# LSH attention and mixture of experts on one core: the hash taken in fp32 from the turned q and k

## The chip, the cores and the metric

The kernel runs on one core of a Trainium2 chip. The metric is the device time of one execution in microseconds (us). The kernel before was timed three times: 741.52, 741.85 and 741.86 us, median 741.85. The core has five engines that matter here, each with its own queue that is worked off in order: TensorE (PE, its weight loads shown as PEld), VectorE (DVE), ScalarE (ACT), GpSimd (POOL) and SyncE (SP), which issues the DMAs.

## What is computed

There are 2 batches, 8 heads, 768 tokens and a head dimension of 64; the experts are 4, with 512 inputs and 1024 hidden units. A token's bucket is made of the signs of six projections of its q (or k), and attention is only between tokens of one bucket:

```python
q_bits = (np.einsum('bhsd,dk->bhsk', q, proj) > 0).astype(np.int64)
k_bits = (np.einsum('bhsd,dk->bhsk', k, proj) > 0).astype(np.int64)
q_bucket = np.sum(q_bits * powers, axis=-1)
k_bucket = np.sum(k_bits * powers, axis=-1)
mask = q_bucket[:, :, :, None] == k_bucket[:, :, None, :]
scores = np.where(mask, scale * np.matmul(q, k.transpose(0, 1, 3, 2)), -1e9)
attn = np.exp(scores - np.max(scores, axis=-1, keepdims=True))
attn = attn / (np.sum(attn, axis=-1, keepdims=True) + 1e-09)
x = np.matmul(attn, v)          # heads side by side: 1536 x 512
# experts, p = domain_probs / (sum + 1e-9)
for e in range(E):
    out += p[:, e:e + 1] * (np.maximum(x @ w1[e], 0.0) @ w2[e])
```

## The kernel before, in words

The sixteen heads are numbered 0 to 15 in the order (batch, head). Each is worked in six tiles of 128 queries; the tiles stand in one sequence of 48 per batch. For every step of the sequence the generator `attention` emits stages of several tiles in the order TXSUVMEYNRP, and every engine's queue keeps that order:

- S: four matmuls into `sps` (two banks of PSUM), the scores of a tile with the mask folded in by extra rows of `al` and `k2`; DVE then takes the row minimum and writes `p` (L391). `sps` has two buffers.
- E: ACT's exponential of the tile before (L407), with the row sum into `den`; the last tile of a head adds 1e-9 to `den` on ACT (L410).
- T (heads 0 to 8, called mixed): six PE transposes of the probabilities into two `ptps` banks, copied out by ACT, or by ACT and DVE (L458, L460). Heads 9 to 15 (light) instead turn 32x32 blocks on DVE (X) and go through a DMA to DRAM and back (`scr`, then `pt` in stage Y).
- V: the product with v, `pv` (L509): fp32 matmuls of 64 columns in pairs, one of a pair at column position 0 and one at 64, `LAG_V` steps after the head's last tile: two blocks of six matmuls at lags 4 and 6 for a mixed head, one of twelve at lag 7 for a light one. U copies `pv` out (`xf`), N takes the reciprocal of `den`, R spreads it by DMA, M multiplies it in on POOL.
- P: one piece of `prep_head` for the next head, a generator that is advanced once per step, so that each of its `yield`s moves what follows to the next tile.

`prep_head` makes the operands of the next head. q and k are loaded with 32-wide blocks side by side and turned by one DVE transpose into `xt` (q in partitions 0 to 63, k in 64 to 127), for the heads in `BLOCKS`; heads 9 and 10 are loaded plainly and turned by six PE transposes into `tps`. Then ACT writes the high part `ah` (scaled, rounded to fp32r, L230), DVE the low part `al` (L231), POOL copies parts of `ah` into `q1` and `k2` (L221). All this is in the head's tile 0. The hash of q and k with `proj` is six matmuls of 108 columns into two `hps` banks (L329): high data with the high and the low part of `proj`, low data with the high part; it stands two tiles later for a mixed head, one tile later for a light one. ACT's Sign (L316) writes the bits into `k2`, POOL scales them into `al` (L343) and copies twelve rows back.

`hps` and `tps` of these heads come from the pool of two double banks that `sps` uses too (tag `big`). The four single banks (tag `one`) serve `ptps`, `pv` and the experts' `mps`. Heads 0 and 1 are prepared by code of their own that the change leaves.

Batch 0 runs alone, with parts of the weights' splits between (DVE cast L683, POOL difference L676). From there the experts' matmuls for batch 0 (`mps`, L715 to L717 and L775 to L777) are emitted with the light heads of batch 1 among them: `prep_head`, S and T yield costs, and the attention is advanced whenever its costs fall behind the experts'. Then the experts for batch 1 run alone. Every DMA, the weights `ws` among them, is issued by SP in the order of emission.

Of the kernel before, what the change touches and what calls it, by code (L numbers as in the profile page):

```python
# [14 lines left out]
P = 128  # L15
# [3 lines left out]
SGN_SCALE = float(2**20)  # L19
ATT_PACE = 1.0  # L20
LAG_E = 1
LAG_N = 3
LAG_R = ((6, 4), (7, 6))
LAG_T = 3
LAG_X = 2
LAG_Y = 4
LAG_V = ((4, 6), (7,))
LAST_V = (4, 5)
LAG_U = (3, 1)
LAG_M = (10, 10)  # L30
PP_BUFS = 6
TW = 3
QK_AT = 1
BLOCKS = (2, 3, 4, 5, 6, 7, 8, 11, 12, 13, 14, 15)
W_LOAD = 14
W_BUFS = 2
WC = 2
# [12 lines left out]
def tile_lsh_attention__then__domain_moe(  # L50
# [59 lines left out]
    pr = const.tile([P, 2, NB], F32, name="pr")  # L110
    phi_t = const.tile([P, P], F32R, name="phi")
    plo_t = const.tile([P, P], F32R, name="plo")
    phi, plo = phi_t[:, :MKE], plo_t[:, :MKE]
    eps = const.tile([P, 1], F32, name="eps")
    warm = const.tile([P, 8], F32, name="warm")
    dp = const.tile([P, B, NT, E], F32, name="dp")
    dsum = const.tile([P, B, NT], F32, name="dsum")
# [2 lines left out]
    def two(t):  # L120
        return t.rearrange("p (a n) -> p a n", a=2)
# [26 lines left out]

    def setup():
        nc.vector.memset(warm, 0.0)  # L150
        nc.vector.memset(eps, 1e-9)
        nc.scalar.activation(warm[:, 0:1], warm[:, 0:1], ACTF.Exp)
        make_identity(nc, ident)
        keep_warm(N_WARM)
        step_column(qk_scale, ((0, -scale), (D, 1.0)))
        step_column(
            sgn_bias, ((0, -TINY), (MQ + NB, TINY), (MQE, 0.0), (MK, TINY), (MK + NB, -TINY), (MKE, 0.0))
        )
        step_column(bit_mul, ((0, 0.5), (MK, BIG / 2)))
        nc.vector.memset(phi_t.bitcast(F32), 0.0)  # L160
        nc.vector.memset(plo_t.bitcast(F32), 0.0)
        for i, s in ((0, -1.0), (1, 1.0)):
            hi, lo = (
                x[:, MQ:P].rearrange("p (a n) -> p a n", a=2)[:, :, i * NB : (i + 1) * NB] for x in (phi_t, plo_t)
            )
            nc.vector.tensor_scalar(out=hi, in0=pr, scalar1=s, scalar2=None, op0=ALU.mult)
            nc.vector.scalar_tensor_tensor(
                out=lo, in0=pr, scalar=s, in1=hi.bitcast(F32), op0=ALU.mult, op1=ALU.subtract
            )
# [17 lines left out]
    def in_blocks(b, h):  # L187
        return b * H + h in BLOCKS

# [99 lines left out]

    def prep_head(b, h):  # L290
        second = (b, h) == (0, 1)
        if not second and not in_blocks(b, h):
            tqk = loaded.pop((0, b, h))
        q1, al, ah, k2 = stack_tiles(b, h)
        if second:
            for ps, sl in zip(in_psum, halves):
                split_half(ah[:, sl], al[:, sl], ps[:, :NH])
        elif in_blocks(b, h):
            if (b, h) not in xts:
                turn_blocks(b, h)  # L300
                yield 0
            split_half(two(ah), two(al), two(xts.pop((b, h))))
        else:
            ps = big("tps")
            for c in range(NT):
                nc.tensor.transpose(
                    ps[:, c // 3, (c % 3) * P : (c % 3 + 1) * P], tqk[:, c].rearrange("p a d -> p (a d)"), ident
                )
            split_half(two(ah), two(al), ps[:, :, :NH])
        for rows in (slice(0, D), slice(D, P)):  # L310
            copy_pool(q1[rows], ah[0:D].bitcast(F32))
        copy_pool(k2[0:D], ah[D:P].bitcast(F32))
        yield 654

        def sign():
            nc.scalar.activation(  # L316
                two(k2[D:MKE]), hps[D:MKE, :, :NH], ACTF.Sign, bias=sgn_bias[D:MKE], scale=SGN_SCALE
            )

        if mixed(b, h) and (second or in_blocks(b, h)):  # L320
            yield 0
        if second:
            ps = [one("hps1") for _ in range(2)]
        else:
            hps = big("hps")
            ps = [hps[:, i] for i in range(2)]
        for j, (w, a) in enumerate(((phi, ah), (plo, ah), (phi, al))):
            for i, sl in enumerate(halves):
                nc.tensor.matmul(ps[i][:MKE, :NH], w, a[:, sl], start=j == 0, stop=j == 2)  # L329
        copy_pool(ah[0:D], al[D:P].bitcast(F32))  # L330
        if second:
            for i, sl in enumerate(halves):
                nc.scalar.activation(
                    k2[D:MKE, sl], ps[i][D:MKE, :NH], ACTF.Sign, bias=sgn_bias[D:MKE], scale=SGN_SCALE
                )
        if not mixed(b, h):
            sign()
        yield 978
        if b and h and not in_blocks(b, h):
            yield 0  # L340
        if mixed(b, h) and not second:
            sign()
        nc.gpsimd.tensor_scalar(  # L343
            out=al[D:MKE],
            in0=k2[D:MKE].bitcast(F32),
            scalar1=1.0,
            scalar2=bit_mul[D:MKE],
            op0=ALU.add,
            op1=ALU.mult,
        )  # L350
        copy_pool(k2[MQ:MQE], al[MK:MKE].bitcast(F32))
        yield 0

    xhi = {}
    xlo = {}
# [46 lines left out]
    def stage_e(b, h, t):  # L402
        pt, nb = probs_t[b, h, t]
        r, o, n = span_of(b, h, t)
        if o == 0:
            dens[b, h, r] = sm.tile([P, NT], F32, tag="den", name="den")
        nc.scalar.activation(pt, pt, ACTF.Exp, bias=nb, scale=-1.0, accum_out=dens[b, h, r][:, o : o + 1])  # L407
        if o == n - 1:
            den = dens[b, h, r][:, :n]
            nc.scalar.activation(den, den, ACTF.Identity, bias=eps)  # L410

    rdbs = {}
    rows = {}
# [1 line left out]
    def stage_n(b, h, t):  # L415
        r, o, n = span_of(b, h, t)
        if o != n - 1:
            return
        den = dens.pop((b, h, r))
        rd = sm.tile([P, NT], F32, tag="rd", name="rd", bufs=2)  # L420
        nc.vector.reciprocal(out=rd[:, :n], in_=den[:, :n])
        rows[b, h, r] = dr.tile([P, n], F32, tag=f"row{n}", name="row", bufs=6)
        nc.sync.dma_start(out=rows[b, h, r], in_=rd[:, :n])
# [149 lines left out]
    def attention():  # L573
# [3 lines left out]
        def do(op, i):  # L577
# [10 lines left out]
            elif op == "T":  # L588
                j = i - LAG_T
                if 0 <= j < n and heavy(*seq[j]):  # L590
                    stage_t(*seq[j])
                    return 654
            elif op == "X":
                j = i - LAG_X
                if 0 <= j < n and not heavy(*seq[j]):
                    stage_x(*seq[j])
            elif op == "Y":
                j = i - LAG_Y
                if 0 <= j < n and j % G == G - 1 and not heavy(*seq[j]):
                    b, h, t = seq[j]  # L600
                    stage_y(b, h, t // G)
            elif op == "S":
                if i < n:
                    b, h, t = seq[i]
                    if t == 0:
                        x = hseq.index((b, h))
                        prep[0] = prep_head(*hseq[x + 1]) if x + 1 < len(hseq) else iter(())
                    stage_s(b, h, t)
                    return 652 + 4270 // NT
                return DRAIN  # L610
            elif op == "V":
                for bh, lag in ended(i):
                    for part, at in enumerate(v_lags(*bh)):
                        if lag == at:
                            stage_v(*bh, part, len(v_lags(*bh)))
            elif op == "U":
                for bh, lag in ended(i):
                    if lag == u_lag(*bh):
                        stage_u(*bh)
            elif op == "M":  # L620
                for (b, h), lag in ended(i):
                    for g in range(NT // G):
                        if h % 2 and lag == (u_lag(b, h) if (b, h) == (0, H - 1) else LAG_M[b] + g):
                            stage_m(b, h, g)
            elif op == "E":
                j = i - LAG_E
                if 0 <= j < n:
                    stage_e(*seq[j])
            elif op == "P":
                if i < n:  # L630
                    b, h, t = seq[i]
                    c = next(prep[0], None) if t >= PREP_AT else None
                    x = hseq.index((b, h))
                    if t == NT - 1 and x + 2 < len(hseq) and in_blocks(*hseq[x + 2]) and mixed(*hseq[x + 2]):
                        turn_blocks(*hseq[x + 2])
                    if t == QK_AT and x + 2 < len(hseq):
                        load_qk(*hseq[x + 2])
                    if t == NT - 1 and x + 1 < len(hseq):
                        load_v(*hseq[x + 1])
                    return c  # L640
# [417 lines left out]
```

## Time and profile before

| what | value |
|---|---|
| median of three runs | 741.85 us |
| the profiled execution | 741.69 us, its span 740.0 us (1.7 us lie around it) |
| PE busy | 720.4 us, 97% of the span |
| PEld, DVE, ACT, POOL busy | 84%, 64%, 40%, 41% |
| the chain that ended last | PE 91%, ACT 4%, DVE 4% |
| waits of PE for another engine, largest | `hps` L329 for DVE p L391, 9.3 us |

"Busy" of PE counts a matmul from its start until its modelled end, so that matmuls that follow each other overlap; what a matmul takes of PE is read from the starts of neighbours. `pv` has two records in the trace for each matmul of the program (384 for 16 heads of twelve). The share of the span is an average over three stages: batch 0's attention alone until about 149 us, the experts of batch 0 with batch 1's attention until about 425 us, and the experts of batch 1.

### The profile page before, as it was taken

What the parts mean: (1) busy time and instruction counts of PE and PEld (TensorE: products, weight loads), DVE (VectorE), ACT (ScalarE), POOL (GpSimd) and SP (SyncE); (2) the same over time, 40 slices, a digit from 0 to 9 for tenths busy, and PEclk for the clock granted to TensorE, in tenths of its full rate; (3) what the DMA queues carried; (4) which work ended last, traced back from release to release, by engine and by line L of the source; (5) the groups of instructions that cost most, each with busy time, mean ns of one, the idle gap of its engine ahead of it and who ended that gap; (6) DMA issues with size and microseconds to landing.
All of it is one profiled execution on the core that took longest, in us unless ns stands there. A gap on an engine that the chain in (4) does not pass through costs nothing.

```text
span 740.0 us, 10166 instructions
## 1 busy us (share of the span) xinstructions
PE 720.4 (97%) x3826; PEld 618.4 (84%) x3826; DVE 474.5 (64%) x781; ACT 298.9 (40%) x592; POOL 306.3 (41%) x279
## 2 busy tenths in 40 slices
PE   8898889999999999999999999999999999999997
PEld 6666666698897897979779799998989989899896
DVE  6677776545776666667553334798668686676863
ACT  6676767643242241523312010443435334353440
POOL 5338585442335441644132324844234242343420
PEclk9999999999999999999999999999999999999999
DMA  6233324302877797789668211242121221212202
GB/s 143 44 65 66 79 43 101 74 13 69 208 203 177 216 229 189 194 209 280 173 196 231 83 58 57 72 157 85 48 67 58 85 86 34 81 57 78 93 0 86
DMA packets 85504, 83.05 MB, mean 112 GB/s; under 512 B 49872, under 2 KB 52432, under 8 KB 85456
## 3 DMA queue, kind: packets, MB, share of 16 engines
q1 hardware_dynamic: 84432, 82.08, 41.0%
q8 instruction: 30, 0.49, 0.3%
q10 hardware_dynamic: 1024, 0.33, 0.2%
q14 instruction: 18, 0.15, 0.1%
HBM read 62.68 MB, written 19.71 MB: 111 GB/s over the span
## 4 chain that ended last, share of the span: by engine, by line
PE 91%; ACT 4%; DVE 4%; issue 0%; DMA 0%; POOL 0%; DVEq 0%; POOLq 0%
PE mps L715 12%; PE mps L716 12%; PE mps L717 12%; PE pv L509 9%; PE mps L776 6%; PE mps L775 6%; PE mps L777 6%; PE sps L384 3%; PE sps L386 3%; PE ptps L454 3%; PE hps L329 3%; PE mps L930 2%; PE mps L926 2%; PE mps L929 2%; DVE al L231 2%; PE pd L926 2%
## 5 line engine op out<-in xcount | busy, mean ns | idle before, releaser
L715 PE MATMUL mps<-w2hi,hh 128*128 128x512 f32 (+1 forms) x388 | 150.7, 388 | 0.0
L717 PE MATMUL mps<-w2hi,hl 128*128 128x512 f32 (+1 forms) x388 | 150.5, 388 | 0.0
L716 PE MATMUL mps<-w2lo,hh 128*128 128x512 f32 (+1 forms) x388 | 150.4, 388 | 0.0
L391 DVE TENSOR_SCALAR_CACHE_REDUCE p<-sps 128x768 f32<-128x768 f32 x96 | 90.4, 943 | 34.0 <-PE sps L386 32.1
L407 ACT ACTIVATE p<-p,nb 128x768 f32<-128x768 f32 x96 | 89.4, 932 | 37.0 <-DVE p L391 36.5
L709 DVE SCALAR_TENSOR_TENSOR acc<-mps,pe,acc 128x512 f32<-128x512 f32 (+1 forms) x85 | 63.0, 742 | 63.1 <-PE mps L717 62.6
L781 ACT ACTIVATE hh<-mps 128x384 fp32r<-128x384 f32 x64 | 31.4, 490 | 162.3 <-PE mps L777 162.3
L776 PE MATMUL mps<-xs,w1hi 128*128 128x384 f32 x256 | 85.9, 336 | 0.6 <-POOL xs L554 0.6
L775 PE MATMUL mps<-xs,w1hi 128*128 128x384 f32 x256 | 86.4, 337 | 0.0
L777 PE MATMUL mps<-xs,w1lo 128*128 128x384 f32 x256 | 85.9, 336 | 0.0
L717 PEld LDWEIGHTS mps<-w2hi,hl 128*128 128x128 f32 x388 | 72.9, 188 | 15.6
L912 POOL TENSOR_TENSOR w2lo<-ws,w2hi 128x512 fp32r<-128x512 f32 x32 | 40.5, 1286 | 108.4 <-ACT w2hi L911 108.4
L716 PEld LDWEIGHTS mps<-w2lo,hh 128*128 128x128 f32 x388 | 72.9, 188 | 13.8
L715 PEld LDWEIGHTS mps<-w2hi,hh 128*128 128x128 f32 x388 | 72.8, 188 | 13.8
L676 POOL TENSOR_TENSOR w1lo<-ws,w1hi 128x512 fp32r<-128x512 f32 x32 | 42.6, 1332 | 88.3 <-DVE w1hi L683 58.8
L782 DVE SCALAR_TENSOR_TENSOR hl<-mps,hh 128x384 fp32r<-128x384 f32 x64 | 35.4, 555 | 66.6 <-ACT hh L781 66.4
L676 POOL TENSOR_TENSOR w2lo<-ws,w2hi 128x512 fp32r<-128x512 f32 x32 | 41.3, 1289 | 70.5 <-DVE w2hi L683 56.3
L509 PE MATMUL pv<-pt,tv 128*64 128x384 f32 x288 | 67.6, 492 | 0.0
L221 POOL TENSOR_SCALAR q<-ah 64x768 fp32r<-64x768 f32 (+1 forms) x33 | 32.2, 975 | 68.5 <-ACT ah L230 67.2
L384 PE MATMUL sps<-ah,q 128*128 128x384 f32 x192 | 54.6, 365 | 0.3 <-DVE p L391 0.3
L454 PEld LDWEIGHTS ptps<-ident,p 128*128 128x128 f32 x324 | 38.7, 145 | 16.3 <-issue 7.8
L871 POOL TENSOR_TENSOR w1lo<-ws,w1hi 128x512 fp32r<-128x512 f32 x24 | 37.1, 1551 | 36.4 <-ACT w1hi L867 22.7
(135 smaller groups left out, 1430.5 us busy)
## 6 DMA issues: line engine op xcount, KB each, us to landing
ws<-in_moe_w_dram SPq DMA_DIRECT2D x64, 512.0 KB, 4.0
scr<-t SPq DMA_DIRECT2D x14, 1152.0 KB, 8.9
pt<-scr SPq DMA_DIRECT2D x56, 288.0 KB, 6.1
tv<-in_v_dram SPq DMA_DIRECT2D x16, 192.0 KB, 4.3
out_dram<-acc SPq DMA_DIRECT2D x11, 256.0 KB, 2.0
rdb<-row SPq DMA_DIRECT2D x14, 192.0 KB, 5.3
tqk<-in_q_dram SPq DMA_DIRECT2D x26, 96.0 KB, 3.3
tqk<-in_k_dram SPq DMA_DIRECT2D x24, 96.0 KB, 3.4
```

Of the source, the lines that this page charges most:

```text
L384: nc.tensor.matmul(ps[:, i, :NH], q1[:, sl], k1[:, i * NH : (i + 1) * NH], start=True, stop=False)
L391: nc.vector.tensor_scalar(out=two(pt), in0=ps[:, :, :NH], scalar1=MASKED, scalar2=MASKED, op0=ALU.min, op1=ALU.min, accum_out=nb,)
L407: nc.scalar.activation(pt, pt, ACTF.Exp, bias=nb, scale=-1.0, accum_out=dens[b, h, r][:, o : o + 1])
L509: nc.tensor.matmul(dst, vvs[b, h][:, c], pts[b, h, g][c], start=c == 0, stop=c == NT - 1, tile_position=(0, g * D),)
L676: nc.gpsimd.tensor_tensor(out=lo[:, c - 1], in0=st[c - 1], in1=hi[:, c - 1].bitcast(F32), op=ALU.subtract)
L709: nc.vector.scalar_tensor_tensor(out=acc, in0=ps, scalar=pcol, in1=acc, op0=ALU.mult, op1=ALU.add)
L715: nc.tensor.matmul(ps, hh[:, ts], w2hi[:, f, cs], start=n == 0, stop=False)
L716: nc.tensor.matmul(ps, hh[:, ts], w2lo[:, f, cs], start=False, stop=False)
L717: nc.tensor.matmul(ps, hl[:, ts], w2hi[:, f, cs], start=False, stop=n == FC - 1)
L775: nc.tensor.matmul(ps[:, :SB], w1hi[:, kk, fs], xhi[b, kk][:, sl], start=kk == 0, stop=False)
L776: nc.tensor.matmul(ps[:, :SB], w1hi[:, kk, fs], xlo[b, kk][:, sl], start=False, stop=False)
L777: nc.tensor.matmul(ps[:, :SB], w1lo[:, kk, fs], xhi[b, kk][:, sl], start=False, stop=kk == KD - 1)
```

## The change

The hash of heads 2 to 15 is no longer taken from the split parts but from `xt` in plain fp32, with a stationary operand `pf` (the signed and scaled `proj`, 44 columns, made once on POOL): two matmuls, one for each half of the tokens, into one bank of the `one` pool at column positions 0 and 64. Two Signs of 384 columns on ACT replace one of 768, the second half of the tokens being read from other partitions (the bias column is copied there). The order in `prep_head` is by two tables: with `SPLIT_AT` the high part and POOL's copies come one tile later for mixed heads (tile 1), the low part always one tile after the high one, and with `HASH_AT` the hash comes in tile 3 of a mixed head and tile 1 of a light one, in stage P and so behind V where V has a block in that step. `LAG_V` of the light heads goes from 7 to 8. Heads 9 and 10 are loaded in blocks and turned on DVE as the others, and `xt` of the light heads too is made in the last tile of the head before the one in which it is used. The 1e-9 is added by a DVE instruction ahead of the reciprocal instead of one on ACT. A head's yields sum to 978 instead of 1632.

PE around the preparation of head 3, in batch 0's attention (`sps` the scores, `ptps` the transposed probabilities, `pv` the product with v). Before:

```order
L386 MATMUL sps<-k_375,al 128x384 x2
L329 MATMUL hps<-ah,phi 128x384 x2
L329 MATMUL hps<-ah,plo 128x384 x2
L329 MATMUL hps<-al,phi 128x384 x2
L454 MATMUL ptps<-ident,p 128x128 x6
L384 MATMUL sps<-ah,q_372 128x384 x2
L386 MATMUL sps<-k_375,al 128x384 x2
L509 MATMUL pv<-pt,tv 64x384
```

And with the change, from the same tile's scores on:

```order
L404 MATMUL sps<-k_377,al 128x384 x2
L470 MATMUL ptps<-ident,p 128x128 x6
L402 MATMUL sps<-ah,q_374 128x384 x2
L404 MATMUL sps<-k_377,al 128x384 x2
L525 MATMUL pv<-pt,tv 64x384
...
L525 MATMUL pv<-pth,tv 64x384
L346 MATMUL hps<-xt,pf 44x384 x2
L470 MATMUL ptps<-ident,p 128x128 x6
```

The six matmuls between the scores of tile 2 and the transposes are gone, and two stand at the end of V's first block instead.

DVE in the same stretch, from the turn of a head's `xt` to its low part `al` (`p` evicts the scores, `pt` and `pth` the transposes, `xf` the product). Before:

```order
L288 STREAM_TRANSPOSE xt<-tqk 128x768
L458 COPY pth<-ptps 128x3x128
L391 TENSOR_SCALAR p,nb<-sps 128x768
L231 SCALAR_TENSOR_TENSOR al<-xt,qk_scale,ah 128x768
L391 TENSOR_SCALAR p,nb<-sps 128x768
L458 COPY pth<-ptps 128x3x128
L391 TENSOR_SCALAR p,nb<-sps 128x768
L536 COPY xf<-pv 64x384
L421 RECIPROCAL rd<-den 128x6
```

With the change:

```order
L299 STREAM_TRANSPOSE xt<-tqk 128x768
L474 COPY pth<-ptps 128x3x128
L409 TENSOR_SCALAR p,nb<-sps 128x768 x2
L474 COPY pth<-ptps 128x3x128
L409 TENSOR_SCALAR p,nb<-sps 128x768
L552 COPY xf<-pv 64x384
L436 TENSOR_SCALAR den<-den 128x6
L437 RECIPROCAL rd<-den 128x6
L333 SCALAR_TENSOR_TENSOR al<-xt,qk_scale,ah 128x768
```

The low part goes from behind the scores of tile 0 to the end of tile 2's work, behind two more evictions of scores.

PE among the experts' matmuls of batch 0, where heads 12 to 15 are prepared; with the change the hash follows a light head's V (for heads 9, 10 and 11 there is no V in that step, and it stands alone):

```order
L733 MATMUL mps<-w2hi,hl 128x512
L525 MATMUL pv<-pt,tv 64x384 x12
L346 MATMUL hps<-xt,pf 44x384 x2
L402 MATMUL sps<-ah,q_2121 128x384 x2
L404 MATMUL sps<-k_2124,al 128x384 x2
```

The twelve matmuls of a light head's V, six pairs, stand in one piece, and the hash, one more pair, directly behind them.

The diff, cut to what the text speaks of:

```diff
+SPLIT_AT = (1, 0)
+HASH_AT = (3, 1)
...
-LAG_V = ((4, 6), (7,))
+LAG_V = ((4, 6), (8,))
...
-BLOCKS = (2, 3, 4, 5, 6, 7, 8, 11, 12, 13, 14, 15)
+BLOCKS = tuple(range(2, 16))
...
+    pf = const.tile([P, P - D], F32, name="pf")
...
+        nc.gpsimd.tensor_copy(sgn_bias[0 : MKE - D], sgn_bias[D:MKE])
...
+            nc.gpsimd.tensor_scalar(
+                out=pf.rearrange("p (a n) -> p a n", a=2)[:, :, i * NB : (i + 1) * NB],
+                in0=pr,
+                scalar1=qk_scale,
+                scalar2=s,
...
     def prep_head(b, h):
         second = (b, h) == (0, 1)
-        if not second and not in_blocks(b, h):
-            tqk = loaded.pop((0, b, h))
         q1, al, ah, k2 = stack_tiles(b, h)
+
+        def copies():
+            for rows in (slice(0, D), slice(D, P)):
+                copy_pool(q1[rows], ah[0:D].bitcast(F32))
+            copy_pool(k2[0:D], ah[D:P].bitcast(F32))
+
         if second:
             for ps, sl in zip(in_psum, halves):
                 split_half(ah[:, sl], al[:, sl], ps[:, :NH])
-        elif in_blocks(b, h):
-            if (b, h) not in xts:
-                turn_blocks(b, h)
-                yield 0
-            split_half(two(ah), two(al), two(xts.pop((b, h))))
-        else:
-            ps = big("tps")
-            for c in range(NT):
-                nc.tensor.transpose(
-                    ps[:, c // 3, (c % 3) * P : (c % 3 + 1) * P], tqk[:, c].rearrange("p a d -> p (a d)"), ident
-                )
-            split_half(two(ah), two(al), ps[:, :, :NH])
-        for rows in (slice(0, D), slice(D, P)):
-            copy_pool(q1[rows], ah[0:D].bitcast(F32))
-        copy_pool(k2[0:D], ah[D:P].bitcast(F32))
-        yield 654
-
-        def sign():
-            nc.scalar.activation(
-                two(k2[D:MKE]), hps[D:MKE, :, :NH], ACTF.Sign, bias=sgn_bias[D:MKE], scale=SGN_SCALE
-            )
-
-        if mixed(b, h) and (second or in_blocks(b, h)):
+            copies()
+            yield 654
             yield 0
-        if second:
             ps = [one("hps1") for _ in range(2)]
-        else:
-            hps = big("hps")
-            ps = [hps[:, i] for i in range(2)]
-        for j, (w, a) in enumerate(((phi, ah), (plo, ah), (phi, al))):
-            for i, sl in enumerate(halves):
-                nc.tensor.matmul(ps[i][:MKE, :NH], w, a[:, sl], start=j == 0, stop=j == 2)
-        copy_pool(ah[0:D], al[D:P].bitcast(F32))
-        if second:
+            for j, (w, a) in enumerate(((phi, ah), (plo, ah), (phi, al))):
+                for i, sl in enumerate(halves):
+                    nc.tensor.matmul(ps[i][:MKE, :NH], w, a[:, sl], start=j == 0, stop=j == 2)
+            copy_pool(ah[0:D], al[D:P].bitcast(F32))
             for i, sl in enumerate(halves):
                 nc.scalar.activation(
                     k2[D:MKE, sl], ps[i][D:MKE, :NH], ACTF.Sign, bias=sgn_bias[D:MKE], scale=SGN_SCALE
                 )
-        if not mixed(b, h):
-            sign()
-        yield 978
-        if b and h and not in_blocks(b, h):
+            yield 978
+        else:
+            xt = xts.pop((b, h))
+            for _ in range(SPLIT_AT[not mixed(b, h)]):
+                yield 0
+            nc.scalar.activation(two(ah), two(xt), ACTF.Copy, scale=qk_scale)
+            copies()
             yield 0
-        if mixed(b, h) and not second:
-            sign()
+            nc.vector.scalar_tensor_tensor(
+                out=two(al),
+                in0=two(xt),
+                scalar=qk_scale,
+                in1=two(ah).bitcast(F32),
+                op0=ALU.mult,
+                op1=ALU.subtract,
+            )
+            copy_pool(ah[0:D], al[D:P].bitcast(F32))
+            for _ in range(HASH_AT[not mixed(b, h)] - SPLIT_AT[not mixed(b, h)] - 1):
+                yield 0
+            hps = one("hps")
+            for i, sl in enumerate(halves):
+                nc.tensor.matmul(
+                    hps[i * D : i * D + MKE - D, :NH],
+                    pf[:, : MKE - D],
+                    xt[:, sl],
+                    start=True,
+                    stop=True,
+                    tile_position=(0, i * D),
+                )
+            for i, sl in enumerate(halves):
+                rows = slice(i * D, i * D + MKE - D)
+                nc.scalar.activation(
+                    k2[D:MKE, sl], hps[rows, :NH], ACTF.Sign, bias=sgn_bias[rows], scale=SGN_SCALE
+                )
+            if not mixed(b, h):
+                yield 978
         nc.gpsimd.tensor_scalar(
             out=al[D:MKE],
             in0=k2[D:MKE].bitcast(F32),
@@ -349,7 +367,7 @@
             op1=ALU.mult,
         )
         copy_pool(k2[MQ:MQE], al[MK:MKE].bitcast(F32))
-        yield 0
+        yield 978 if mixed(b, h) and not second else 0
...
-        if o == n - 1:
-            den = dens[b, h, r][:, :n]
-            nc.scalar.activation(den, den, ACTF.Identity, bias=eps)
...
+        nc.vector.tensor_scalar(out=den[:, :n], in0=den[:, :n], scalar1=1e-9, scalar2=None, op0=ALU.add)
         nc.vector.reciprocal(out=rd[:, :n], in_=den[:, :n])
...
-                    if t == NT - 1 and x + 2 < len(hseq) and in_blocks(*hseq[x + 2]) and mixed(*hseq[x + 2]):
+                    if t == NT - 1 and x + 2 < len(hseq) and in_blocks(*hseq[x + 2]):
                         turn_blocks(*hseq[x + 2])
```

## Rows read from the trace of the kernel before

**Rows 1.** Windows (us): start:end, length, busy us (instructions) PE PEld DVE ACT POOL, PEclk, DMA share, GB/s.

```profile
53.60:71.60 18.00, 15.76 (x93) 11.61 (x92) 12.74 (x24) 11.65 (x26) 15.07 (x15) 0.91 0.23 55
87.10:102.60 15.50, 14.21 (x92) 10.20 (x91) 12.34 (x23) 11.48 (x25) 12.38 (x13) 1.00 0.20 40
107.00:107.50 0.50, 0.40 (x1) 0.40 (x2) 0.50 (x4) 0.42 (x1) 0.50 (x1) 0.50 0.00 0
120.40:135.10 14.70, 14.09 (x92) 10.26 (x91) 9.40 (x21) 11.85 (x26) 11.27 (x12) 1.00 0.27 71
...
21.30:135.10 113.80, 102.67 (x629) 75.33 (x627) 79.74 (x152) 80.75 (x169) 66.80 (x69) 0.96 0.31 65
200.00:250.00 50.00, 50.00 (x265) 44.09 (x264) 34.98 (x60) 17.14 (x34) 22.39 (x21) 1.00 0.82 202
```

**Rows 2.** Chain that ended last, around one head's preparation: start us, us, what.

```profile
87.06 0.84 ACT ah L230
...
87.92 1.68 DVE al L231
89.60 0.89 DVE p L391 x2
...
90.53 1.30 PE hps L329 x6
```

**Rows 3.** Waits from 20 to 150 us: total us, times, longest us.

```profile
PE hps L329 <- DVE p L391: 9.3, 7, 2.1
...
PE ptps L454 <- ACT pth L460: 1.9, 6, 0.3
```

**Rows 4.** Timeline of PE around the hash: start us, us, instruction, idle before.

```profile
90.53 0.60 PE L329 MATMUL hps<-ah,phi 128*108 128x384 f32 x2 [0.97 <-DVE p L391]
...
91.67 0.81 PE L454 MATMUL ptps<-ident,p 128*128 128x128 f32 x6
...
107.10 0.97 PE L329 MATMUL hps<-ah,phi 128*108 128x384 f32 x2 [1.94 <-DVE p L391]
...
137.22 0.60 PE L329 MATMUL hps<-ah,phi 128*108 128x384 f32 x2 [0.80 <-DVE al L231]
```

**Rows 5.** Timeline of PE from behind one V block to behind the next.

```profile
95.40 0.87 PE L454 MATMUL ptps<-ident,p 128*128 128x128 f32 x6
...
98.25 0.54 PE L509 MATMUL pv<-pt,tv 128*64 128x384 f32 x1
...
100.34 0.87 PE L454 MATMUL ptps<-ident,p 128*128 128x128 f32 x6
```

**Rows 6.** Timeline of PE in the second stage.

```profile
154.74 0.82 PE L306 MATMUL tps<-ident,tqk 128*128 128x128 f32 x6
155.32 0.42 PE L775 MATMUL mps<-xs,w1hi 128*128 128x384 f32 x1
...
163.04 0.50 PE L329 MATMUL hps<-ah,phi 128*108 128x384 f32 x2
...
164.08 0.34 PE L775 MATMUL mps<-xs,w1hi 128*128 128x384 f32 x1
...
254.16 0.34 PE L777 MATMUL mps<-xs,w1lo 128*128 128x384 f32 x1
254.43 4.09 PE L509 MATMUL pv<-pt,tv 128*64 128x384 f32 x24
258.45 0.62 PE L384 MATMUL sps<-ah,q 128*128 128x384 f32 x2
```

**Rows 7.** Instructions of hps and their readers: ns min/median/max.

```profile
L316 ACT ACTIVATE k<-hps,sgn_bias x14: 895/896/903, 29.2 to 336.6; 44x768 fp32r<-44x768 f32 x14
...
L333 ACT ACTIVATE k<-hps,sgn_bias x2: 564/570/575, 14.1 to 14.5; 44x384 fp32r<-44x384 f32 x2
```

**Rows 8.** Groups of DVE from 21 to 135 us: busy us, mean ns.

```profile
L179 DVE TENSOR_SCALAR dsum<-dsum 128x12 f32<-128x12 f32 x1 | 0.2, 173 | 0.0
```

**Rows 9.** Waits of SP's queue, whole span: total us, times, longest us.

```profile
SPq L491 <- PE pv L509: 33.5, 6, 7.5
```

More of the change, by code (lines that the diff above doesn't have):

```diff
@@ L112, in tile_lsh_attention__then__domain_moe @@
     plo_t = const.tile([P, P], F32R, name="plo")
+    pf = const.tile([P, P - D], F32, name="pf")
     phi, plo = phi_t[:, :MKE], plo_t[:, :MKE]
-    eps = const.tile([P, 1], F32, name="eps")
     warm = const.tile([P, 8], F32, name="warm")
@@ L150, in setup @@
         nc.vector.memset(warm, 0.0)
-        nc.vector.memset(eps, 1e-9)
         nc.scalar.activation(warm[:, 0:1], warm[:, 0:1], ACTF.Exp)
@@ L161, in setup @@
         nc.vector.memset(plo_t.bitcast(F32), 0.0)
+        nc.gpsimd.memset(pf, 0.0)
         for i, s in ((0, -1.0), (1, 1.0)):
@@ L164, in setup @@
                 x[:, MQ:P].rearrange("p (a n) -> p a n", a=2)[:, :, i * NB : (i + 1) * NB] for x in (phi_t, plo_t)
+            )
[5 more added lines that the diff above has]
+                op0=ALU.mult,
+                op1=ALU.mult,
             )
@@ L335, in prep_head @@
                 )
-        if not mixed(b, h):
-            sign()
-        yield 978
-        if b and h and not in_blocks(b, h):
-            yield 0
-        if mixed(b, h) and not second:
-            sign()
+            yield 978
[5 more added lines that the diff above has]
+            copies()
+            yield 0
+            nc.vector.scalar_tensor_tensor(
[3 more added lines that the diff above has]
+                in1=two(ah).bitcast(F32),
+                op0=ALU.mult,
+                op1=ALU.subtract,
[17 more added lines that the diff above has]
+                    k2[D:MKE, sl], hps[rows, :NH], ACTF.Sign, bias=sgn_bias[rows], scale=SGN_SCALE
+                )
+            if not mixed(b, h):
+                yield 978
         nc.gpsimd.tensor_scalar(
```

## The prediction, as it was put on record

> **What bounds the kernel now.** I read the page's shares first, then windows over the stages, then the chain of waits, then PE's timeline. PE is the bound, but not in the same way everywhere. In the second stage every window looks like [rows 1]'s last: PE busy 50.00 of 50 us, DVE 35, ACT 17; PE stands still nowhere to speak of, so there only work taken off PE counts. In batch 0's attention (21.3 to 135.1 us) PE is busy 102.7 of 113.8 us with the ends as modelled, and the reader is to see where it stands still: the chain [rows 2] goes ACT's high part, DVE's low part (1.68 us), DVE's eviction of the scores, and only then the hash on PE. DVE works in order, so the scores of tile 1 wait behind the low part, and the hash needs the double bank that these scores hold. PE loses 0.3 to 2.1 us a head to it, 9.3 us in seven heads, and 1.9 us more on transposes behind the same piece of ACT work [rows 3]. In three of the seven heads the granted clock then falls: a window right behind such a stop shows 0.50, the 1.2 GHz level, a head with it takes 18.0 us at a mean of 0.91, one without 15.5 [rows 1]. The first two of the six hash matmuls show 0.97 us there instead of 0.60; at full clock the six take 1.14 (90.53 to 91.67) [rows 4].
>
> **What a hash of two fp32 matmuls costs.** `pv` has the form: 384 columns of fp32, stationary 64 wide, positions 0 and 64 of one bank. A light head's V is twelve matmuls in the program and 24 records in the trace: 254.43 to 258.45 us, 4.02 us [rows 6]. That is six pairs, 0.67 us each; the start comes 0.27 behind the last record before it, where such a record takes 0.17, so about 0.28 of it all is the change into this form and out again, and a pair alone is (4.02 - 0.18) / 6 = 0.64 us. So a hash takes 0.64 us behind a V and 0.64 + 0.28 = 0.92 us alone. The six fp32r matmuls took 1.04 among the experts' (163.04 to 164.08) [rows 6]. The stationary operand has 44 columns and not 64, which I cost at nothing. Bounds from rows: 0.33 us, if it went as one pair of records; 1.28, if the halves went one behind the other.
>
> The Trainium skill (FP8 and Floating Point Precision, TensorE Precision Notes) says that true fp32 makes four passes through the array, which speaks against this change: an fp32r matmul takes 0.173 us here, so four passes of one half would be 0.69 and of two halves 1.39, above the 1.14 of the six. The trace agrees with the four passes and adds that two halves at positions 0 and 64 together take 0.67; by the rule without the pairing 14 hashes would cost some 10 us more than I count. The skill's TensorEngine Tiling (Key Properties) says that changing the tiling mode drains the engine; the 0.28 us around V agrees.
>
> **The change part by part, batch 0's attention (heads 2 to 8).** Behind a V block, two tiles of transposes and scores take PE 98.25 - 95.40 = 2.85 us, and a V block 100.34 - 98.25 = 2.09 [rows 5]. A head without a stop is 3 x 2.85 + 2 x 2.09 + 0.64 = 13.4 us. Seven are 93.6 against 113.8 now: 20.2 us at most. By parts: stops 9.3, transposes 1.9, matmuls 7 x (1.14 - 0.64) = 3.5, clock 3 x (1 - 0.91) x 18 = 4.9, together 19.6; the rest is rounding and short gaps.
>
> What is late next? The low part now stands at the end of tile 2, ahead of V's first block and the hash: 2.7 us in which PE needs nothing from DVE but what it has, so its 1.6 us are mostly covered. If not, the transposes of tile 4 wait for a single bank. ACT's high part moves behind tile 1 and delays its copies of tile 2 by 0.9. The Signs are 2 x 0.57 against 0.90 [rows 7], and stand ahead of the copies of tile 4, which have until the transposes of tile 5. DVE gains an add (a wider one: 0.17 us [rows 8]), ACT loses one. POOL makes the bits after the Signs and has until the next head's scores, two tiles and a V block or 4.9 us later. So all come near to the new 13.4 us: DVE is busy 12.3 in a head with casts of weights, plus 0.17, and 9.4 in one without; ACT 11.5 to 11.9; POOL 12.4, 11.3 and in one head 15.1, 1.7 too much [rows 1]. With queues in order and this full I do not expect the floor. I take back 1.7 us in that head, 0.8 in the three others with casts (what DVE's 12.5 leaves free of 13.4) and 0.4 in the last three: 5.3. Ends: nothing taken back, or all stops of 11.2 us with the clock's loss. **Net 14.9 us.**
>
> **Heads 9 to 15.** Head 9, at the end of the first stage: transposes 0.58 (154.74 to 155.32) plus 0.09 for the slower start of what follows [rows 6], hash 1.13, stop 0.80 [rows 4], less 0.92, since no V stands there: 1.6. Head 10: 0.67 + 1.04 - 0.92 = 0.8. Head 11: 0.1. Heads 12 to 15: 4 x (1.04 - 0.64) = 1.6, PE being full. **Together 4.1 us.** Two turns more on DVE and ACT's halved Signs lie under PE: DVE is at 35 of 50, ACT at 17 [rows 1]. The `one` bank that a hash holds until its Signs are done is one of four; PE would have to wait for a bank if ACT were late by more than two of the experts' products (twelve matmuls of 0.17 us each). Setup on POOL and the smaller yields (the attention gets ahead of the experts a little) I cost at nothing; the bound is 0.5 us either way.
>
> **Sum.** 741.69 - 14.9 - 4.1 = 722.7 us; the profiled execution is 0.16 below the median, so I say **723 us**.
>
> **Rivals.**
> 1. *The stops move instead of going.* The low part, evictions and casts are the same work for DVE, and a stop reappears ahead of tile 4, or at tile 3's transposes, with the clock's fall behind it. Then only matmuls go: 3.5 us, and 4.1 - 0.8 = 3.3: 741.85 - 6.8 = 735. For it: DVE at 12.5 of 13.4 us in heads with casts, and POOL's 15.1. Against it: the block of PE work that needs no DVE now follows the low part directly; before, none did.
> 2. *No stop at all:* 741.85 - 20.2 - 4.1 = 717.5. For it: in the walk above no engine exceeds 13.4. Against it: full queues.
> 3. *The halves of the hash go one behind the other* (1.28 us): 14 x 0.64 = 9 us more, 731. Against it: `pv` has this form.
> 4. *Slower: SP's queue.* With V a step later in light heads, the DMA of the next head's turned probabilities (stage Y) stands in SP's queue ahead of the V that frees its buffer. SP already waits there for V, 33.5 us in six waits, up to 7.5 [rows 9]. Behind it are the weights, DVE's casts in order behind those, and the evictions of scores behind the casts. If a step more cost PE a stop of today's mean wait, 33.5 / 6 = 5.6 us, in each of six heads, it would be 34 us on the forecast: 757. It decides from 19 / 6 = 3.2 us of stop a head. Against it: what stands behind the waiting DMA mostly waits for PE to get to the same place, and PE has free banks for two products of the experts ahead.
>
> **How the numbers follow.** The forecast has 0.55, with its own range 718 to 729; rival 1 0.25 (its upper end 741); rival 2 0.09; rival 3 0.04; rival 4 0.07, two thirds of it slower than before. The range for 8 in 10 is 716 to 736. A difference below 0.2% (1.5 us) is no change that this measurement can tell. Faster by more: 0.92 (all but the upper end of rival 1 and rival 4); same 0.03; slower 0.05.
>
> **What would show it.** Right: the window from 21 to 135 us shrinks by 13 to 18 us, PEclk is 1.00 in it, the waits list has no PE wait of 9 us, the hash records start right behind `pv` and take 0.64 us; the second stage is shorter by 2 to 3 us with PE still full. Wrong: waits of `ptps` or `sps` for DVE or ACT of 1 us a head, a window at 0.50, hash records in a row and not in pairs, or PE waiting for DVE casts that wait for weights behind SP's Y.

## The result, and the profile after

The kernel with the change took 729.26 us (median of 4 runs, 729.12 to 729.58), the kernel before on the same chip 741.68 us. The ratio of the means is 0.9844, 95% interval 0.9815 to 0.9873; by the medians it is faster by 12.4 us. The forecast was 723 us with a range of 716 to 736. The kernel before varies from run to run: in the three sets of runs that go with the experiments its median was 738.91, 738.68 and 740.52 us, and against these the gain would be 9.4 to 11.3 us. The profiled execution has a span of 727.4 us.

Both programs can be cut at one mark, the first product of the experts that waits for POOL's `xs` (the `mps` record with 0.6 us of idle before it). It stands at 151.50 us before and 133.19 after. So the first stage became 18.3 us shorter (forecast: 14.9 and head 9's 1.6, together 16.5), and all that follows became 5.7 us longer (forecast: 2.5 shorter).

Windows of after: first from head 2's preparation to just behind head 9's hash, then one head from V to V and one from hash to hash, then all behind the mark. The columns are those of [rows 1].

```profile
21.30:119.90 98.60, 96.87 (x625) 67.05 (x624) 84.96 (x166) 81.11 (x170) 65.09 (x70) 1.00 0.36 75
24.20:37.77 13.57, 13.57 (x90) 9.53 (x92) 10.63 (x21) 11.35 (x25) 6.01 (x8) 1.00 0.34 63
53.32:67.92 14.60, 13.90 (x90) 9.54 (x88) 11.77 (x24) 11.39 (x25) 13.30 (x14) 1.00 0.29 78
133.19:727.40 594.21, 584.46 (x2990) 512.31 (x2990) 374.75 (x586) 191.96 (x370) 218.77 (x172) 1.00 0.42 121
```

And before, all behind its mark:

```profile
151.50:740.00 588.50, 584.69 (x3008) 517.23 (x3008) 371.16 (x577) 192.70 (x372) 221.02 (x172) 1.00 0.43 121
```

In the first stage PE is busy 96.9 of 98.6 us and the granted clock is 1.00, where [rows 1] had 102.7 of 113.8 and 0.96 (that window ended ahead of head 9's hash, so the two stretches are about 2 us apart in what they hold). Behind the mark PE is busy as long as before (584.5 against 584.7), but 9.75 us of the stretch are not PE's, where 3.8 were.

The chain that ended last, around head 2's hash (start, us, what), answers to [rows 2]. No other engine stands in it:

```profile
24.20 2.09 PE pv L525 x12
26.28 0.65 PE hps L346 x4
26.93 0.81 PE ptps L470 x6
```

PE's timeline there (start, us, instruction) answers to [rows 4]. Each fp32 matmul has two records, so four are the pair; from the start of the hash to the start of the transposes behind it are 0.75 us, and the chain has 0.65:

```profile
26.11 0.81 PE L346 MATMUL hps<-xt,pf 128*44 128x384 f32 x4
26.86 0.87 PE L470 MATMUL ptps<-ident,p 128*128 128x128 f32 x6
```

PE's waits in the first stage (20 to 133 us: total us, times, longest), in place of the 9.3 and 1.9 us of [rows 3]:

```profile
PE ptps L470 <- DVE pt L474: 1.0, 1, 1.0
PE sps L404 <- POOL k L232: 0.6, 1, 0.6
PE ptps L470 <- ACT k L356: 0.5, 1, 0.5
```

Waits behind the mark, of PE, of DVE and of SP's queue:

```profile
PE mps L791 <- DVE hl L798: 4.7, 1, 4.7
PE sps L402 <- DVE p L409: 1.5, 2, 1.2
...
DVE w2hi L699 <- DMA ws<-in_moe_w_dram: 20.1, 4, 8.8
...
SPq L507 <- PE pv L525: 45.5, 6, 11.2
```

Before, PE had none of the first two, SP waited 33.5 us for V [rows 9], and DVE waited for `ws` only this long:

```profile
DVE w2hi L683 <- DMA ws<-in_moe_w_dram: 7.8, 3, 3.6
```

The chain of after shows how they hang together, here at two light heads' V:

```profile
264.85 4.07 PE pv L525 x24
268.93 0.29 SPq L507
...
270.74 0.38 SPq L496
271.16 10.02 DMA ws<-in_moe_w_dram
281.27 0.43 DVE w2hi L699
...
284.36 0.96 DVE p L409 x2
...
361.35 4.07 PE pv L525 x24
...
368.39 9.13 DMA ws<-in_moe_w_dram
...
377.62 0.14 DVE w2hi L699
...
377.96 0.56 DVE hl L798
...
378.56 0.66 PE mps L791
```

Read it downward: SP's queue holds the loads of the next head's turned probabilities (L507), which want the buffer that V (L525) frees. The weights `ws` stand behind them and start when V has ended. They then take 10.02 and 9.13 us; four loads of `pt`, a store of `t` and four loads of `tqk` are issued around the first of them between 268.9 and 280.8 us. Such landing times are not new in this stage: from 150 to 420 us the median `ws` load lands after 6.8 us before (longest 11.5) and 7.3 after (longest 11.4), while over the whole program it is 4.0 in both. What is new is how long before them DVE gets to its cast. DVE waits for them with its cast `w2hi`; behind the cast stand the eviction of scores `p` and the experts' `hl`, and PE stands still for 4.7 us at the second place. After that stop the granted clock is at its 1.2 GHz level until 382 us: 0.50 from 379 to 382 us, 0.98 from 382 to 383.

### The profile page after: what moved, and what is told of

The parts are those of the page before. It is cut to its first block, busy times and chain, and to the rows that moved or that the text cites. A ratio compares the mean times of both kernels' runs of the same rounds, so it can differ in the third digit from the quotient of the medians.

```text
span 727.4 us, 10195 instructions
## 1 busy us (share of the span) xinstructions
PE 711.5 (98%) x3786; PEld 602.5 (83%) x3786; DVE 483.0 (66%) x800; ACT 296.6 (41%) x588; POOL 303.0 (42%) x283
## 4 chain that ended last, share of the span: by engine, by line
PE 88%; DVE 3%; DMA 3%; ACT 2%; POOL 1%; issue 1%; SPq 1%; DVEq 0%; POOLq 0%; ACTq 0%
PE mps L731 12%; PE mps L732 12%; PE mps L733 12%; PE pv L525 8%; PE mps L791 5%; PE mps L792 5%; PE mps L793 5%; PE ptps L470 4%; PE sps L404 4%; PE sps L402 4%; DMA ws<-in_moe_w_dram 3%; PE mps L946 2%; PE mps L942 2%; PE mps L945 2%; PE pd L942 2%; PE pa L946 2%
## 5 line engine op out<-in xcount | busy, mean ns | idle before, releaser
L791 PE MATMUL mps<-xs,w1hi 128*128 128x384 f32 x256 | 87.6, 342 | 4.7 <-DVE hl L798 4.7
L792 PE MATMUL mps<-xs,w1hi 128*128 128x384 f32 x256 | 86.6, 338 | 0.6 <-POOL xs L570 0.6
L525 PE MATMUL pv<-pt,tv 128*64 128x384 f32 x288 | 67.3, 492 | 0.0
L791 PEld LDWEIGHTS mps<-xs,w1hi 128*128 128x128 f32 x256 | 48.6, 190 | 8.2 <-DVE hl L798 5.0
L470 PEld LDWEIGHTS ptps<-ident,p 128*128 128x128 f32 x324 | 36.4, 140 | 18.3 <-ACT p L425 8.2
```

The source lines that it names most:

```text
L470: nc.tensor.transpose(ps[:, c * P : (c + 1) * P], pt[:, (a + c) * P : (a + c + 1) * P], ident)
L525: nc.tensor.matmul(dst, vvs[b, h][:, c], pts[b, h, g][c], start=c == 0, stop=c == NT - 1, tile_position=(0, g * D),)
L791: nc.tensor.matmul(ps[:, :SB], w1hi[:, kk, fs], xhi[b, kk][:, sl], start=kk == 0, stop=False)
L792: nc.tensor.matmul(ps[:, :SB], w1hi[:, kk, fs], xlo[b, kk][:, sl], start=False, stop=False)
```

## The experiments

The question was where the second stage lost 8.2 us (5.7 longer, where 2.5 shorter was forecast). Theory A: V a step later (`LAG_V` 8) holds up SP, and so the weights. Theory B: the attention, whose yields sum to 978 a head and no longer 1632, runs ahead of the experts differently; or the hash itself does it. Edits are to the kernel after unless another is named; times are medians, "rest" is the span behind the mark.

**V's lag alone.** Two runs: the change with the old lag, and the kernel before with the new one.

```diff
-LAG_V = ((4, 6), (8,))
+LAG_V = ((4, 6), (7,))
```

> The changed kernel with the light heads' V back at lag 7 and nothing else undone, so that the hash of heads 12 to 15 stands alone instead of behind V. The changed kernel took 729.3 us; its first stage ends 18.3 us earlier than before, and what follows is 5.7 us longer where 2.5 us less was forecast, 8.2 us apart. Theory A (the later V makes SP wait longer ahead of the weights, DVE's casts wait for them and PE for DVE): the 8.2 us go, four changes of the matmul form at 0.28 us come: 722 us, and no wait of PE mps for DVE hl of 4.7 us. Theory B (the loss is from the smaller yields, the two turns more on DVE or the hash's bank): 729.3 + 1.1 = 730 us.

721.84 us, ratio to before 0.9765 (0.9738 to 0.9791). First stage 133.09, rest 587.0: 1.5 shorter than before and 7.2 shorter than with lag 8. PE has no stop for `hl`. The waits are back at or near those of before (SP for V, DVE for `ws`):

```profile
SPq L507 <- PE pv L525: 30.2, 6, 6.6
...
DVE w2hi L699 <- DMA ws<-in_moe_w_dram: 7.7, 4, 3.4
```

The two loads that the chain of after showed land no faster here: after 10.1 us (issued at 268.23) and 9.3 us (issued at 362.18), against 10.0 and 9.1. But DVE's casts wait for them for 1.12 and 3.44 us instead of 4.85 and 8.79:

```profile
278.41 0.43 DVE L699 CAST w2hi<-ws 128x512 fp32r<-128x512 f32 x1 [1.12 <-DMA ws<-in_moe_w_dram]
371.58 0.43 DVE L699 CAST w2hi<-ws 128x512 fp32r<-128x512 f32 x1 [3.44 <-DMA ws<-in_moe_w_dram]
```

So the lag makes the weights start too late; it does not make them slow.

> The kernel before with LAG_V of the light heads 8 instead of 7 and nothing else. Theory A (the later V alone makes the loss of the second stage): 741.8 + 8 = 750 us, with DVE waiting for weights and PE for DVE. Theory B (the loss needs other parts of the change): 741.8 us within 0.5.

The kernel before with lag 8 took 746.55 us, ratio 1.0095 (1.006 to 1.0131), slower. Its rest is 595.6 us against 588.5, 7.1 longer, though it has none of the change's hash or yields. It shows the same three waits:

```profile
SPq L491 <- PE pv L509: 49.7, 6, 10.7
...
DVE w2hi L683 <- DMA ws<-in_moe_w_dram: 19.3, 6, 9.2
...
PE mps L775 <- DVE hl L782: 4.1, 1, 4.1
```

So the lag costs 7 us by itself, with the change (7.2) and without it (7.1); theory B falls. The first stage of this run ended at 148.72 and not 151.50, with code that is the same there: one fall of the clock in it, not three.

**The way it costs.** First the waiting loads were put a step later, so that they no longer stand ahead of V.

```diff
-LAG_Y = 4
+LAG_Y = 5
```

> The changed kernel with the light heads' stage Y one step later too (LAG_Y 5 instead of 4), so that the DMA that needs V's buffer is issued behind that V again, while V and the hash stay where they are. Theory A (it is SP's wait ahead of the weights): 729.3 - 8.2 = 721 us, SP's waits for pv back to some 33 us in six. Theory B (it is something else, as V's own place): 729 us.

727.58 us, ratio 0.9844 (0.9817 to 0.9872), rest 592.5. The forecast of this run failed. DVE's waits for `ws` did fall from 20.1 to 8.2 us and the stop for `hl` went, but the loads that now start late are late themselves, and V waits for them (in the chain they take 9.99 and 9.87 us). Behind the longer of these waits the granted clock falls, to 0.50 from 209 to 211 us:

```profile
PE pv L525 <- DMA pt<-scr: 3.5, 2, 2.5
```

Then the weights were taken out of SP's queue, with lag 8 and, as a control, with lag 7:

```diff
-        nc.sync.dma_start(out=t, in_=src.rearrange("(k p) f -> p k f", p=P))
+        nc.gpsimd.dma_start(out=t, in_=src.rearrange("(k p) f -> p k f", p=P))
```

> The kernel after (LAG_V 8 for light heads), with the weights' DMAs (ws) issued from GpSimd's queue instead of SyncE's, so that no weight stands behind a DMA that waits for V. Theory A (the lost time of the second stage is weights that start late behind SP's wait for V): DVE's waits for ws shrink below 10 us, PE's stop for hl (4.7 us) goes, the time behind the first stage's mark falls from 594 to about 587, total 721 to 723 us. Theory B (a step more of V's lag costs PE in another way, as by the order of the matmuls): the time stays at 728 to 730. Theory C (the weights are late because their transfers are slow beside the other DMAs, whoever issues them): DVE still waits 20 us for ws, 728 to 731. If GpSimd issues slowly or holds up its own work, all of them are a few us longer; the run with lag 7 and the same edit gives that price.

> LAG_V 7 for light heads and the weights' DMAs issued from GpSimd: the price of GpSimd's queue by itself. Theory A: at lag 7 SP's wait costs nothing (721.8 us with SP), so this run shows the queue's own price alone, 0 to 3 us: 721 to 725; and the run with lag 8 and the same edit is within 1.5 us of it. Theory B: the lag still costs 7 us between the two runs.

Lag 8: 721.13 us, ratio 0.974 (0.9715 to 0.9765), rest 585.75. Lag 7: 722.48 us, ratio 0.9755 (0.9734 to 0.9776), rest 587.2. With lag 8:

```profile
SPq L507 <- PE pv L525: 36.9, 6, 8.9
...
DVE w2hi L699 <- DMA ws<-in_moe_w_dram: 2.9, 2, 2.7
```

SP still waits 36.9 us for V, but weights no longer stand behind that, and PE's only wait behind the mark is the 0.6 us at it. That is theory A: the 8.1 us between 729.26 and 721.13 are weights held up in one queue behind a load that waits for V. At lag 7 GpSimd's queue costs 0.64 us (722.48 - 721.84; the two were timed on different chips, and by the spans behind the mark it is 0.2), so the held weights cost 8.1 + 0.64 = 8.8 us. The lag gives back 1.35 of it (722.48 - 721.13) by putting the hash behind V, and what is left, 7.4, is the difference between lag 8 and lag 7 with SP (729.26 - 721.84). The transfers are hardly faster from GpSimd (median landing from 150 to 420 us 6.5 us against 7.3, over the whole program 4.4 against 4.0): they start in time.

**The hash behind V or alone.** With lag 7 and the hash in tile 1, the hash of heads 12 to 15 stands alone. Here it is issued in tile 0, ahead of the low part, where V now is:

```diff
-LAG_V = ((4, 6), (8,))
+LAG_V = ((4, 6), (7,))
...
+            if not mixed(b, h):
+                hash_now()
             yield 0
             nc.vector.scalar_tensor_tensor(
...
```

> The changed kernel with V of the light heads at lag 7 and their hash in tile 0, ahead of the low part, so that heads 12 to 15 have it behind V again. Theory A: 721 us (the 8.2 us of the second stage go, nothing is paid for the form). Theory B: 729 us.

720.7 us, ratio 0.9751 (0.9719 to 0.9783), rest 585.7: 2.8 shorter than before (forecast of the prediction for the second stage: 2.5). It is 1.1 us under the run with lag 7 alone, for four hashes that priced 0.28 less each behind V, 4 x 0.28 = 1.1. The pair of runs with GpSimd's queue shows the same step, made by moving V instead of the hash (722.48 to 721.13). This run has the lowest time here, below both kernels; the 0.4 us to lag 8 with GpSimd's queue, timed on another chip, decide nothing.

**The pair.** With lag 7, the two halves of the hash in two banks at column position 0 each:

```diff
-            hps = one("hps")
+            hps = [one("hps") for _ in range(2)]
...
-                    hps[i * D : i * D + MKE - D, :NH],
+                    hps[i][: MKE - D, :NH],
...
-                    tile_position=(0, i * D),
+                    tile_position=(0, 0),
...
```

> The changed kernel with V at lag 7 (721.84 us; its first stage ends at 133.1 us), and with both halves of a hash at column position 0, in two banks, instead of at 0 and 64 of one. Theory A (two fp32 matmuls at 0 and 64 run side by side, 0.65 us for the two): unpaired they take 1.3 us, 0.65 more in 14 heads, 9 us where PE is full in both stages: 731 us, first stage to 137.6. Theory B (the pair gains nothing, a hash takes 0.65 either way): 722 us.

728.17 us, ratio 0.9865 (0.9839 to 0.9891): 6.3 us over its base. The mark stands at 135.83, 2.7 later, for seven hashes that stand behind V and head 9's. PE's timeline around head 2's hash:

```profile
26.38 1.45 PE L346 MATMUL hps<-xt,pf 128*44 128x384 f32 x4
27.76 0.87 PE L469 MATMUL ptps<-ident,p 128*128 128x128 f32 x6
```

1.38 us from start to start, where the pair took 0.75 (26.11 to 26.86). So the halves at positions 0 and 64 run beside each other. By the starts 14 x 0.63 = 8.8 us were to be expected; 6.3 came: 3.6 of 3.8 behind the mark, but 2.7 of 5.0 ahead of it. That the longer hash gives DVE, ACT and POOL time there that they were short of is argued, not shown.

**The place and the parts in the first stage.** All three have lag 7 as base, whose mark is 133.09.

```diff
-SPLIT_AT = (1, 0)
-HASH_AT = (3, 1)
+SPLIT_AT = (0, 0)
+HASH_AT = (2, 1)
```

This moves the high and the low part a tile earlier as well as the hash.

> V at lag 7 (721.84 us, first stage to 133.1), and for heads 2 to 8 the high part in tile 0, the low part in tile 1 and the hash in tile 2, by itself and not behind V. Theory A (the stop of PE is gone because the fp32 hash asks nothing of DVE and takes no double bank, wherever it stands): only the change of form comes, 7 x 0.28 = 2 us: 724 us, first stage to 135. Theory B (the place counts: the low part ahead of V's block, so that DVE's 1.6 us are covered): stops of about 1 us a head come back at scores or transposes, and a clock fall or two: 729 to 733 us, first stage to 141 or more.

726.41 us, ratio 0.984 (0.9814 to 0.9866), mark 137.64, 4.55 later. The hash of mixed heads is then not behind V (7 x 0.28 = 2.0), and the rest is waits of transposes behind DVE's work:

```profile
PE ptps L470 <- DVE pth L474: 3.0, 6, 1.2
```

The low part in the same tile as the high one, hash left where it is:

```diff
             copies()
-            yield 0
             nc.vector.scalar_tensor_tensor(
...
             copy_pool(ah[0:D], al[D:P].bitcast(F32))
+            yield 0
```

> V at lag 7 (721.84 us, first stage to 133.1), and the low part in the same piece as the high part (tile 1 of heads 2 to 8, tile 0 of the light ones), the hash where it is. Theory A of the run with the hash in tile 2: within 1 us, 722 to 723. Theory B (the low part's own step counts, since DVE, in order, waits for ACT's high part and then holds the scores back 1.6 us with no V to cover it): 1 us a head in the first stage, 729 us.

726.41 us, ratio 0.984 (0.9814 to 0.9866), mark 137.82, 4.7 later. DVE's and ACT's work then piles up in one tile:

```profile
PE ptps L470 <- ACT pth L476: 2.1, 6, 0.4
PE pv L525 <- DVE pth L474: 1.6, 3, 0.6
PE ptps L470 <- DVE pt L474: 1.3, 2, 0.9
```

Both lie between what the theories gave. The step from high to low part is worth about as much as the places of the other run: neither is spare.

Last, the old six matmuls from the split parts at the new place:

```diff
-            hps = one("hps")
+            hps = [one("hps") for _ in range(2)]
+            for j, (w, x) in enumerate(((phi, ah), (plo, ah), (phi, al))):
+                for i, sl in enumerate(halves):
+                    nc.tensor.matmul(hps[i][:MKE, :NH], w, x[:, sl], start=j == 0, stop=j == 2)
...
```

> V at lag 7 (721.84 us, first stage to 133.1), with the six fp32r matmuls of before in two single banks at the new place, behind V's block, instead of the two fp32 ones. Theory A (the new place and the step between the parts took the stop away): PE has 1.04 - 0.65 = 0.4 us more a hash in 14 heads, about 5 us: 727 us, first stage to 136. Theory B (the fp32 hash took it away, since the six wait for the low part and hold two single banks): stops come back on top, 733 us or more, first stage to 141.

742.65 us, ratio 1.0072 (1.0042 to 1.0101), mark 141.05, rest 599.7. The rest is 12.7 us longer than its base, since the six need the low part, which a light head has in the same step:

```profile
PE hps L346 <- DVE al L333: 12.2, 7, 2.3
```

Of the 12.2 us, 10.7 lie behind the mark, in heads 10 to 15. In heads 2 to 8, where the low part is done before the hash, PE does not wait for it, and the mark at 141.05 is 10.5 us ahead of the one before (151.50, with three falls of the clock; 7.7 ahead of the 148.72 with one). So in the first stage the new places bring about half of the gain even with the old matmuls. In the light heads the gain hangs on a hash that needs `xt` and nothing of DVE's split.

## Why the prediction was right, and where it missed

**The bound.** PE, with the stops and the clock's falls behind them as the loss of the first stage: right. The stops went (9.3 and 1.9 us to 2.1 us together) and with them every fall in the first stage.

**The hash's price.** 0.64 us behind V: the chain has 0.65. Alone 0.92: head 10's, among the experts' products, takes 1.05 us from the start of the product ahead of it to the next (141.87, 142.14, 142.92), less that product's own 0.17 that is 0.88, and 0.99 with the slower start of the product after it (143.20, 0.28 behind and not 0.17). The 0.18 in (4.02 - 0.18) / 6 is not worked out there, but the V blocks of six and of three pairs bear it out: 4.02 and 2.09 us make 0.64 a pair and 0.16 besides. The 1.38 us of the unpaired run is what four passes of two halves would take, as the Trainium skill (FP8 and Floating Point Precision, TensorE Precision Notes) has it for true fp32: the forecast's 1.39 by that rule. The pairing is why it did not speak against the change, and rival 3 is out (its 731 us are 731.7 by its own terms).

**Heads 2 to 8: forecast 14.9, measured 17.1.** From the scores that both traces have at 21.7 us, ahead of head 2's hash, to head 9's scores in tile 1 it is 21.73 to 135.46 before and 21.67 to 117.68 after, 17.7 us less, of which 0.67 are head 9's transposes. A head takes 13.6 us where POOL has room (floor 13.4) and 14.6 in the two with casts and the product's scaling together. The take-back of 5.3 us was too much; 20.2 - 17.1 = 3.1 came true. The 17.1 are taken against the trace in which the kernel before had three falls of the clock, the one the forecast was made from; at some 1.4 us a fall (last section; priced at 1.6) a trace with one fall would give about 14.3. Its place was right: PE waits in the head whose POOL is full, with a stop of 0.65 us behind POOL's copy `k`:

```profile
61.16 0.62 PE L404 MATMUL sps<-k,al 76*128 76x384 f32 x2 [0.65 <-POOL k L232]
```

So neither rival 1 (the stops move) nor rival 2 (none at all) came, but the likeliest case, nearer to rival 2.

**Head 9: forecast 1.6, measured 1.2** (18.3 - 17.1). The forecast's own terms add up to 1.68 and not 1.6. Transposes and hash save 1.9 and 0.7 is given back ahead of the mark: the transposes behind the hash wait 0.5 us for ACT's second Sign.

**The second stage: forecast 2.5 shorter, 5.7 longer.** The step that failed is rival 4: "Against it: what stands behind the waiting DMA mostly waits for PE to get to the same place, and PE has free banks for two products of the experts ahead." The mechanism was laid out rightly (SP's load waits for V, weights behind it, DVE's casts behind those, evictions behind the casts), but it was priced as all or nothing: a stop of 5.6 us in each of six heads, or none. What came are stops of PE at two places, 1.5 us and 4.7 us with the clock's fall behind it, 8.8 us in sum by the runs. (The trace has 6.2 us of stops, and the eleven products from 378.56 to 382.15 us take 3.59 us where at 0.17 each they take 1.9: about 7.9 together, an estimate.) And the price went by SP's wait for V alone (33.5 us before, 45.5 after) and not by how late the weights behind it then come for DVE, which waits 20.1 us for them instead of 7.8. They land no more slowly than with lag 7, where nothing is lost; they start too late. The prediction's last sign of being wrong, PE waiting for casts that wait for weights behind SP's stage Y, is what came. Without this the sum holds: 720.7 us with lag 7 and the hash behind V, against 723 forecast.

**The total.** It lies in the range although the second stage went the other way: the first stage gave 1.8 us more than was counted (18.3 against 16.5), and the range had been drawn wide enough for most of rival 1. That the number holds is in part luck.

**Yields and setup, costed at nothing:** right, as far as the run with lag 7 shows (rest 1.5 us shorter than before with the hash alone, forecast 2.5 less 1.1).

## What to carry to other kernels

When a step is moved later, look at what waits for it in every queue, the DMA issuer's above all, and count what is queued behind that wait: when it can then start, how long it takes to land in that stretch of the program, and when its reader wants it. A matmul that needs only an early operand may stand anywhere; that freedom was worth more here (stops and clock) than the matmul time that it saved. Where two halves of a small fp32 product fit at column positions 0 and 64, issue them as a pair, directly behind work of the same form.

## What the runs showed of the hardware

The 1e-9 was moved to DVE and priced 0.17 us by [rows 8]. It takes 0.16 to 0.94 us in the second stage, and ends when an instruction of POOL ends: at 282.32 it stands beside a difference of POOL that began at 281.94 and ran to 283.22; at 247.05, with POOL idle, it takes 0.16. Timelines of after, DVE's add and POOL's instruction beside it:

```profile
282.32 0.93 DVE L436 TENSOR_SCALAR den<-den 128x6 f32<-128x6 f32 x1
```

```profile
281.94 1.28 POOL L692 TENSOR_TENSOR w2lo<-ws,w2hi 128x512 fp32r<-128x512 f32 x1 [9.14 <-DVE w2hi L699]
```

The same is seen at 311.09 (0.94, POOL until 312.02) and 380.24 (0.87, POOL until 381.09). The Trainium skill (SBUF — State Buffer, section SBUF: two separate sides) says that a DVE instruction in a 2-port performance mode, or with two inputs from SBUF, shares a pair of ports with GpSimd, and that whichever starts first has the pair for its whole length while the other is blocked. The trace agrees in the times; in which mode the add works no run here shows. The reciprocal is not held up: at 218.04 it took 0.19 us beside a difference of POOL that ran from 217.98 to 219.28.

The kernel before varies by chance where the one after does not: its runs here lie between 736.4 and 742.3 us, the four of after within 0.5 us. The profile of before shows three falls of the clock in the first stage, that of before with lag 8 one, with the same code there and 2.8 us between the marks (151.50 and 148.72): some 1.4 us a fall, an estimate.
